# Attention, MLP and a Sinkhorn-gated MoE on one core: the right side of SBUF moved by 32 bytes, and TensorE's order in the MoE written out by hand

## The chip, the core and the metric

One core of a Trainium2 chip. Times are device microseconds of one execution of the whole program, and the lower the better. A profiled execution is recorded by the hardware profiler; its span is the stretch from the first to the last recorded instruction.

## The reference

Three layers, one after the other, in fp32:

```python
# attention: batch 4, 8 heads, 576 tokens, head width 64, mask by blocks of 64
scores = scale * np.matmul(q, k.transpose(0, 1, 3, 2))
scores = np.where(block_i >= block_j, scores, -1000000000.0)
attn = softmax(scores)
x = (attn @ v), heads side by side            # 2304 tokens x 512
# MLP: w_in 512 x 2048, w_out 2048 x 512
h = x @ w_in
x = np.maximum(0.01 * h, h) @ w_out
# MoE: 8 experts, w1 512 x 1024, w2 1024 x 512, every token in every expert
P = np.exp(x @ w_gate - max)                  # 2304 x 8
for _ in range(8):
    P /= P.sum(1, keepdims=True) + 1e-09
    P /= P.sum(0, keepdims=True) + 1e-09
    P *= N / E
for e in range(E):
    out += P[:, e:e + 1] * (np.maximum(x @ w1[e], 0.0) @ w2[e])
```

## The kernel before

Every fp32 matrix is split into a high and a low part (`...h`, `...l`), and one product is three matmuls: high by high, high by low, low by high. ScalarE (ACT) casts the high part, VectorE (DVE) subtracts to get the low one. The attention takes the first 250 us, the MLP the time up to about 676 us, and the MoE the rest.

**The MLP.** `hidden` (L492) multiplies a block of w_in with 512 or 384 tokens (five blocks of tokens: three of 512, two of 384), `second` (L514) adds the product with w_out into four PSUM banks.

**The MoE.** The tokens come in three passes p of 768, each in two halves of 384. A group (p, e, i) is a pass, an expert e of 8 and a quarter i of its hidden width: 96 groups. In a group the 2 x 2 block product x @ w1 is done with seven block products and sums instead of eight, named by the weight that they use: A11, S1, S2, S4, S3, A12, A22. Each is six matmuls (L672) of 128 x 384 into a PSUM bank. Bank X takes A11, S2, S3, A22 in turn, Y takes S1 and S4, Z takes A12. Between them ScalarE copies X (`s1`, `s2`) and Y (`s5`) out of PSUM, and VectorE adds such a copy to a later state of a bank: c12 = Y + s2, c11 = Z + s1, c22 = X + s5. From these ScalarE and VectorE make the high and low part of h11, h12, h22 (relu); h21 comes from X after A22. So A22 has to come after c22 has read X, S2 after s1, S3 after s2, S4 after s5.

Two groups share one `combine`, for each of six tiles of 128 tokens: twelve matmuls 128 x 512 (L708) that multiply h with w2, into one of the o banks; VectorE then adds the bank, weighted by the gate, to `xa` (L721).

Weights come by SP's queue into raw buffers (`wraw`, two of them for w1 and w2 together): `w1_load` and `w2_load` issue the DMA, which waits until the buffer's last reader is done. POOL makes the sums of w1's blocks (`one`, `two`), ScalarE casts w1h and w2h, VectorE subtracts w1l and w2l. `x_step` splits one of the seven x operands of a pass (`xhS..`, `xlS..`, ScalarE L659 and VectorE L660), five of them after a subtraction on POOL or from x itself; at the last group of a pass it makes those of the next pass. The eight rounds of the gate's normalisation (`rows`, `columns`) run in the first groups of the MoE; `columns` has a small matmul with `ones` that needs `cs` from VectorE, and its bank is read into `cr`.

The framework's scheduler sets the order of each engine's instructions, from the order in which the code emits them and its own estimates of their length. `alloc_tile_pool(..., side="right")` places a pool from the upper end of SBUF downward; other pools lie on the left side. On the right lie the split x of the attention and MLP (`xh`, `xl`), later the split x of the MoE (`xpart`) and h11, h12, h21 (`hpool1`).

Of the kernel before, what the change touches and what calls it, by code (L numbers as in the profile page):

```python
# [8 lines left out]
F32 = mybir.dt.float32  # L9
# [27 lines left out]
def block_attention_mlp_moe(  # L37
# [37 lines left out]
    const = ctx.enter_context(tc.tile_pool(name="const", bufs=1))  # L75
    xpool = tc.alloc_tile_pool(name="xpool", bufs=1, side="right")
# [452 lines left out]
    turn_o = [0]  # L529
# [6 lines left out]
    def gate_part(p, t0, n, ps):  # L536
        for t in range(t0, t0 + n):
            for c in range(KC):
                nc.tensor.matmul(  # L539
                    ps[:, t * E:(t + 1) * E], xv[p][:, c, t * P:(t + 1) * P], gate[:, c, :],  # L540
                    start=c == 0, stop=c == KC - 1,
                )

    def gate_take(p, ps):
# [4 lines left out]
    def gate_pass(p):  # L549
        ps = ps_h.tile([P, 512], F32, name="l_ps", tag="h")  # L550
        gate_part(p, 0, TC, ps)
        gate_take(p, ps)
# [51 lines left out]
    def w1_steps(n):  # L604
        if n >= NGR:
            return []
        _, e, i = groups[n]
        t = {}

        def sums():  # L610
            raw = w_raw.pop((1, NG + e, i)).rearrange("p (c f) -> p c f", c=KC)
            a11, a12, a21, a22 = (raw[:, c:c + 2, f:f + P] for f in (0, P) for c in (0, 2))
            one, two = (
                rawpool.tile([P, 512], F32, name="wa", tag="wa").rearrange("p (s c f) -> p s c f", s=2, c=2)
                for _ in range(2)
            )
            nc.gpsimd.tensor_tensor(out=one[:, 0], in0=a21, in1=a22, op=ALU.add)  # L617
            nc.gpsimd.tensor_tensor(out=one[:, 1], in0=one[:, 0], in1=a11, op=ALU.subtract)  # L618
            nc.gpsimd.tensor_tensor(out=two[:, 0], in0=a11, in1=a21, op=ALU.subtract)  # L619
            nc.gpsimd.tensor_tensor(out=two[:, 1], in0=a12, in1=one[:, 1], op=ALU.subtract)  # L620
            for k in "SA":
                for s in "hl":
                    t[k + s] = w1pool.tile([P, 1024], F32R, name=f"w1{s}", tag=f"w1{s}").rearrange(
                        "p (s c f) -> p s c f", s=4, c=2
                    )
            t["raw"], t["one"], t["two"] = raw, one, two
            for s, (k, j) in {"S1": "S0", "S2": "S1", "S3": "S2", "S4": "S3",
                              "A11": "A0", "A12": "A1", "A22": "A2"}.items():
                wq[n, s] = (t[k + "h"][:, int(j)], t[k + "l"][:, int(j)])

        def part(k, a, b, src):
            def run():
                x = src()
                hi, lo = t[k + "h"][:, a:b], t[k + "l"][:, a:b]
                if k == "A" and b - a == 2:
                    hi, lo = (y.rearrange("p s c f -> p (s c) f") for y in (hi, lo))
                elif k == "A":
                    hi, lo = hi[:, 0], lo[:, 0]
                nc.scalar.copy(out=hi, in_=x)  # L639
                nc.vector.tensor_tensor(out=lo, in0=x, in1=f32(hi), op=ALU.subtract)  # L640
            return run

        return [
            sums,
            part("A", 0, 2, lambda: t["raw"][:, :, 0:P]),
            part("A", 2, 3, lambda: t["raw"][:, 2:4, P:2 * P]),
            part("S", 0, 2, lambda: t["one"]),
            part("S", 2, 4, lambda: t["two"]),
        ]
# [14 lines left out]

    def product(n, k, name, first):
        if first:
            bank[n, name] = ps_h.tile([P, 512], F32, name="h_ps", tag="h")
        ps = bank[n, name][:, 0:HT]
        (wh, wl), (bh, bl) = wq.pop((n, k)), bq[groups[n][0], k]
        for c in range(2):  # L670
            for s, (w, x) in enumerate(((wh, bh), (wh, bl), (wl, bh))):
                nc.tensor.matmul(  # L672
                    ps, w[:, c], x[:, c], start=first and c == 0 and s == 0, stop=c == 1 and s == 2,
                    skip_group_check=True,
                )
# [19 lines left out]

    def combine(n, t):
# [50 lines left out]
    for m, (e, b, f) in enumerate(todo):  # L747
# [11 lines left out]
        if last and e + 1 == NG:  # L759
            if f == 1:  # L760
                w1_load(0)
                w2_load(0)
            if f == 3:
                for s in w1_steps(0):
                    s()
                w1_load(1)
        if e == 0 and b == 0:
            if f < len(late):
                bits_load(*late[f])
            if 0 < f <= len(late):  # L770
# [15 lines left out]
    hpool1 = tc.alloc_tile_pool(name="hpool1", bufs=3, side="right", reuse_waits="tile")  # L786
    mpool = tc.alloc_tile_pool(name="mpool", bufs=1, reuse_waits="tile")
# [5 lines left out]
    g_ps = {}  # L793

    def gate_last(t0):
        if t0 == 0:
            g_ps[0] = o_bank()
        gate_part(2, t0, 2, g_ps[0])
        if t0 + 2 == TC:
            gate_take(2, g_ps[0])  # L800

    for k in terms:
        x_step(0, k)

    def tail(n):
        product(n, "A22", "X", False)
        quarter(n, "21", "X", None)
        if groups[n][0] + 1 < NPASS and groups[n][1:] == (E - 1, NI - 1):
            x_step(groups[n][0] + 1, "A22")

    for n, (p, e, i) in enumerate(groups):
        turn = p + 1 < NPASS and (e, i) == (E - 1, NI - 1)
        if n >= 2:
            back = n - 2 - n % 2
            units = [lambda t=t: combine(back, t) for t in (range(TC // 2, TC) if n % 2 == 0 else range(TC // 2))]
        elif n == 0:
            units = [lambda t0=t0: gate_last(t0) for t0 in (0, 2, 4)]
        else:
            units = [lambda: None] * 3
        prep = w1_steps(n + 1)  # L820

        def prepare(m):
            for s in prep[:m]:
                s()
            del prep[:m]

        def normal():
            if n and norm:
                norm.pop(0)()

        def done(k):
            if turn:
                x_step(p + 1, k)
# [10 lines left out]
        prepare(1)  # L844
        normal()
        units[1]()
        prepare(1)
        product(n, "S1", "Y", True)
        keep(n, "Y", "s5")
        done("S1")  # L850
        product(n, "S2", "X", False)
        keep(n, "X", "s2")
        prepare(1)
        normal()
        units[2]()
        prepare(2)
        w1_load(n + 2)
        normal()
        product(n, "A12", "Z", True)
        quarter(n, "11", "Z", "s1")  # L860
        done("A12")
        done("S2")
        product(n, "S4", "Y", False)
        quarter(n, "12", "Y", "s2")
        done("S4")
        product(n, "S3", "X", False)
        quarter(n, "22", "X", "s5")
# [39 lines left out]
```

## Time and profile before

| | us |
|---|---|
| median of 3 runs | 2213.59 (2213.29 to 2216.33) |
| the profiled execution | 2214.53 |
| its span | 2212.7 |
| TensorE busy | 2185.7 (99%) |
| VectorE busy | 1320.0 (60%) |
| ScalarE busy | 899.5 (41%) |
| POOL busy | 471.9 (21%) |

A busy share says how long an engine had an instruction in it. Matmuls follow one another before the one ahead has left the array, so their recorded lengths overlap; what a matmul takes of the time is seen from one start to the next.

### The profile page before, as it was taken

To read this page: it belongs to the slowest core of one execution; us is meant where nothing else is said; L and a number is where in the kernel's file an instruction comes from. 1 tells how busy PE (TensorE), PEld (TensorE's weight loads), DVE (VectorE), ACT (ScalarE), POOL (GpSimd) and SP (SyncE) were. 2 spreads that over 40 slices of the span, in tenths; PEclk is the share of its full clock that TensorE was granted. 3 is DMA by queue.
4 is the path that set the end of the run, shared out by engine and by line. 5 is a ranking of instruction groups with operands and counts; after the bars stand their busy time and mean duration, and the time that the engine had idled before them with its cause. 6 is when DMAs were issued, how large, how long until landed. Compare 5 with 4: busy or idle time off the path is not lost.

```text
span 2212.7 us, 29298 instructions
## 1 busy us (share of the span) xinstructions
PE 2185.7 (99%) x10992; PEld 1932.6 (87%) x10992; DVE 1320.0 (60%) x2429; ACT 899.5 (41%) x1902; POOL 471.9 (21%) x547
## 2 busy tenths in 40 slices
PE   7999999999999999999999999999999999999999
PEld 6787777988899988898889888888898888888888
DVE  7999776333237856555557555555557555555554
ACT  6777422332124433443344334433444344334432
POOL 3433322000004121212123212121213121212120
PEclk9999999999999999999999999999999999999999
DMA  4333134010001212221222122212222222122211
GB/s 103 88 85 84 44 115 143 21 56 1 1 20 58 66 58 77 67 67 58 77 67 96 58 77 67 68 57 77 67 68 81 81 68 67 58 76 67 68 57 39
DMA packets 157246, 146.61 MB, mean 66 GB/s; under 512 B 62640, under 2 KB 126128, under 8 KB 157104
## 3 DMA queue, kind: packets, MB, share of 16 engines
q1 hardware_dynamic: 157104, 144.75, 22.2%
q8 instruction: 86, 1.41, 0.3%
q14 instruction: 56, 0.46, 0.1%
HBM read 135.81 MB, written 8.91 MB: 65 GB/s over the span
## 4 chain that ended last, share of the span: by engine, by line
PE 83%; POOL 0%; ACT 0%; DVE 0%; issue 0%; POOLq 0%; ACTq 0%
PE o L708 36%; PE h_ps L672 32%; PE h_ps L492 7%; PE o L514 7%; PE l_ps L539 1%; PE o L539 0%; POOL xa L657 0%; POOL wa L618 0%; POOL wa L617 0%; PE o L574 0%; POOL wa L619 0%; ACT xhS L659 0%; DVE xa L721 0%; DVE w1l L640 0%; ACT w1h L639 0%
## 5 line engine op out<-in xcount | busy, mean ns | idle before, releaser
L708 PE MATMUL o<-w2h,h 128*128 128x512 f32 x2304 | 767.6, 394 | 0.0
L708 PEld LDWEIGHTS o<-w2h,h 128*128 128x128 f32 x2304 | 431.6, 188 | 82.0
L708 PE MATMUL o<-w2l,h 128*128 128x512 f32 x1152 | 455.4, 396 | 0.0
L617 POOL TENSOR_TENSOR wa<-wraw 128x256 f32<-128x256 f32 x96 | 101.5, 1057 | 1394.6 <-DVE w1l L640 1305.6
L721 DVE SCALAR_TENSOR_TENSOR xa<-o,pr,xa 128x512 f32<-128x512 f32 x264 | 193.2, 746 | 172.1 <-PE o L708 172.0
L690 ACT ACTIVATE h<-c 128x384 fp32r<-128x384 f32 x288 | 151.2, 525 | 323.3 <-DVE c L685 318.1
L672 PE MATMUL h_ps<-xhS,w1h 128*128 128x384 f32 x768 | 261.4, 341 | 2.0 <-ACT xhS L659 2.0
L672 PE MATMUL h_ps<-xhS,w1l 128*128 128x384 f32 x768 | 261.4, 340 | 0.0
L672 PE MATMUL h_ps<-xlS,w1h 128*128 128x384 f32 x768 | 261.2, 340 | 0.0
L640 DVE TENSOR_TENSOR w1l<-wa,w1h 128x512 fp32r<-128x512 f32 x192 | 125.5, 695 | 213.1 <-ACT w1h L639 213.1
L708 PEld LDWEIGHTS o<-w2l,h 128*128 128x128 f32 x1152 | 216.2, 188 | 38.0
L639 ACT CAST w1h<-wa 128x512 fp32r<-128x512 f32 x192 | 109.6, 618 | 330.4 <-PE h_ps L672 326.2
L119 DVE TENSOR_TENSOR w2l<-wraw,w2h 128x1024 fp32r<-128x1024 f32 x100 | 127.6, 1276 | 176.0 <-ACT w2h L118 176.0
L679 ACT COPY s<-h_ps 128x384 f32<-128x384 f32 x288 | 136.9, 475 | 158.6 <-PE h_ps L672 158.6
L672 PE MATMUL h_ps<-xhA,w1h 128*128 128x384 f32 x576 | 195.5, 339 | 0.0
L672 PE MATMUL h_ps<-xlA,w1h 128*128 128x384 f32 x576 | 195.5, 339 | 0.0
L672 PE MATMUL h_ps<-xhA,w1l 128*128 128x384 f32 x576 | 195.5, 339 | 0.0
L685 DVE TENSOR_TENSOR c<-h_ps,s 128x384 f32<-128x384 f32 x288 | 160.0, 556 | 46.6 <-ACT h L690 25.7
L691 DVE SCALAR_TENSOR_TENSOR h<-c,h 128x384 fp32r<-128x384 f32 x288 | 158.7, 551 | 0.2
L672 PEld LDWEIGHTS h_ps<-xhS,w1h 128*128 128x128 f32 x768 | 144.9, 189 | 8.5 <-ACT xhS L659 2.3
L672 PEld LDWEIGHTS h_ps<-xlS,w1h 128*128 128x128 f32 x768 | 144.9, 189 | 7.9
L672 PEld LDWEIGHTS h_ps<-xhS,w1l 128*128 128x128 f32 x768 | 145.0, 189 | 1.9
(131 smaller groups left out, 3666.4 us busy)
## 6 DMA issues: line engine op xcount, KB each, us to landing
wraw<-in_moe_w_dram SPq DMA_DIRECT2D x192, 512.0 KB, 3.7
wraw<-in_moe_w_in_dram SPq DMA_DIRECT2D x16, 512.0 KB, 3.9
wraw<-in_moe_w_out_dram SPq DMA_DIRECT2D x16, 512.0 KB, 3.6
out_dram<-xa SPq DMA_DIRECT2D x18, 256.0 KB, 2.0
qraw<-in_q_dram SPq DMA_DIRECT2D x32, 128.0 KB, 2.5
kraw<-in_k_dram SPq DMA_DIRECT2D x32, 128.0 KB, 2.7
vz<-in_v_dram SPq DMA_DIRECT2D x32, 128.0 KB, 2.4
s_in<-wa SPq DMA_DIRECT2D x8, 256.0 KB, 3.1
```

The source lines that it names most:

```text
L119: nc.vector.tensor_tensor(out=lo, in0=raw, in1=f32(hi), op=ALU.subtract)
L492: nc.tensor.matmul(ps[:, 0:n], w[:, c, cols], x, start=c == 0 and s == 0, stop=c == KC - 1 and s == 2,)
L514: nc.tensor.matmul(o_ps[s][:, 0:n], w[:, cut], h[:, 0:n], start=f == 0 and m == 0, stop=f == FC - 1 and m == 2)
L639: nc.scalar.copy(out=hi, in_=x)
L640: nc.vector.tensor_tensor(out=lo, in0=x, in1=f32(hi), op=ALU.subtract)
L672: nc.tensor.matmul(ps, w[:, c], x[:, c], start=first and c == 0 and s == 0, stop=c == 1 and s == 2, skip_group_check=True,)
L679: nc.scalar.copy(out=t, in_=bank[n, name][:, 0:HT])
L685: nc.vector.tensor_tensor(out=c, in0=x, in1=part[n, add], op=ALU.add)
L690: nc.scalar.activation(out=hi, in_=x, func=AF.Relu)
L691: nc.vector.scalar_tensor_tensor(out=lo, in0=x, scalar=0.0, in1=f32(hi), op0=ALU.max, op1=ALU.subtract)
L708: nc.tensor.matmul(o, h, w, start=m == 0, stop=m == 11)
L721: nc.vector.scalar_tensor_tensor(out=a, in0=o, scalar=pr[:, tt, e:e + 1], in1=a, op0=ALU.mult, op1=ALU.add)
```

## The change

- A tile of 8 floats (32 bytes) is placed first on the right side, so that all that follows on that side lies 32 bytes lower.
- In the MoE TensorE's instructions follow the order of the code: `in_order` puts each `product`, `combine` and the gate's last pass behind the last matmul of the one before (`issue_after`). The other engines' order stays with the scheduler.
- The order in a group: A11, S1, A22 of the group before, S2, S4, S3, A12. After an even group (i even, not the first of a pass) come the six combines of the two groups before it. In the last group of a pass A22 of the same group follows A12, and the combines of the group before and this one follow that, with the next pass's x_steps between them. Before, combines stood three to a group between the products, and the scheduler could move them.
- PSUM: the banks of the products go round over five (`h_bank`), those of the combines over three (`o_bank`); before it was four and four.
- `s1` has a pool of its own with two buffers. The two parts of w1 (`w1_a`, `w1_s`) have tiles made separately, at other places in the group; w2's split and the next w2's load stand at the group's end instead of behind A11. The gate of pass 3 is one piece in front of the first group instead of three pieces inside it.

```diff
+    edge = tc.alloc_tile_pool(name="edge", bufs=1, side="right")
+    edge.tile([P, 8], F32, name="edge")
...
     def o_bank():
-        s = turn_o[0] % 4
+        s = turn_o[0] % 3
...
+    def h_bank():
+        turn_h[0] += 1
+        if turn_h[0] % 5 == 0:
+            return ps_o.tile([P, 512], F32, name="o3", tag="o3")
+        return ps_h.tile([P, 512], F32, name="h_ps", tag="h")
...
+    last_mm = [None]
+
+    def in_order(f):
+        def run(*a):
+            with ExitStack() as order:
+                if last_mm[0] is not None:
+                    order.enter_context(tc.issue_after(last_mm[0]))
+                ins = f(*a)
+            last_mm[0] = ins.ins if hasattr(ins, "ins") else ins
+        return run
...
+    order = [*range(TC // 2, TC), *range(TC // 2)]
     for n, (p, e, i) in enumerate(groups):
...
         product(n, "A11", "X", True)
         keep(n, "X", "s1")
-        done("A11")
-        w2_split(n)
-        w2_load(n + 1)
-        normal()
-        units[0]()
-        if n:
-            tail(n - 1)
...
+        product(n, "S1", "Y", True)
+        keep(n, "Y", "s5")
+        if (e, i) != (0, 0):
+            tail(n - 1)
+        w1_a(n + 1)
+        w1_load(n + 2)
+        if 0 < n < 6:
+            normal()
+            normal()
+        product(n, "S2", "X", False)
+        keep(n, "X", "s2")
+        product(n, "S4", "Y", False)
+        quarter(n, "12", "Y", "s2")
+        product(n, "S3", "X", False)
+        quarter(n, "22", "X", "s5")
+        if 0 < n < 6:
+            normal()
+            normal()
+        product(n, "A12", "Z", True)
+        quarter(n, "11", "Z", "s1")
         w2_split(n)
         w2_load(n + 1)
-        normal()
-        units[0]()
...
+        w1_sums(n + 2)
+        if turn:
+            tail(n)
+            back = n - 1
+        elif i % 2 == 0 and (e, i) != (0, 0):
+            back = n - 2
+        else:
+            back = None
+        if back is not None:
+            for m, t in enumerate(order):
+                combine(back, t)
+                if turn and p + 1 < NPASS:
+                    for k in terms[2 * m:2 * m + 2]:
+                        x_step(p + 1, k)
+                if m == 1:
+                    w1_s(n + 2)
+        else:
+            w1_s(n + 2)
...
```

What the scheduler makes of it, at three places. First ScalarE in the middle of a pass, from the cast of a group's w2 (`w2h`) to the copy `s2` of the next, even group; now:

```order
L121 CAST w2h_11168<-wraw_11077 128x1024
L693 COPY s1_11098<-h_ps_11091 128x384
L704 ACTIVATE h11_11070<-c11_11068 128x384
L693 COPY s5_11107<-o3_11100 128x384
L646 CAST w1h_11118<-wraw_11029 128x512
L646 CAST w1h_11118<-wraw_11029 128x256
L704 ACTIVATE h21_11115<-h_ps_10996 128x384
L693 COPY s2_11132<-h_ps_11091 128x384
```

and before:

```order
L118 CAST w2h_10362<-wraw_10225 128x1024
L679 COPY s1_10219<-h_ps_10212 128x384
L690 ACTIVATE h22_10209<-c22_10207 128x384
L639 CAST w1h_10256<-wa_10250 128x512
L639 CAST w1h_10256<-wa_10251 128x512
L690 ACTIVATE h21_10247<-h_ps_10075 128x384
L679 COPY s5_10283<-h_ps_10276 128x384
L679 COPY s2_10291<-h_ps_10212 128x384
```

Between the cast of w2 and `s2` stand the same kinds of operation; the cast of w1's A part (from `wraw`) has come in for that of its S part (from `wa`), and h11 for h22.

Second VectorE at the first turn, from c12 of the last group of pass 1 to the low part of its h22; now:

```order
L699 TENSOR_TENSOR c12_10459<-o3_10419,s2_10451 128x384
L671 TENSOR_TENSOR xlS4_10578<-xa1_2967,xhS4_10577 128x768
L699 TENSOR_TENSOR c22_10470<-h_ps_10410,s5_10426 128x384
L671 TENSOR_TENSOR xlS1_10529<-xa1_2967,xhS1_10528 128x768
L699 TENSOR_TENSOR c11_10482<-h_ps_10475,s1_10417 128x384
L705 SCALAR_TENSOR_TENSOR h12_10461<-c12_10459,h12_10461 128x384
L647 TENSOR_TENSOR w1l_10557<-wa_10493,w1h_10556 128x512
L647 TENSOR_TENSOR w1l_10557<-wa_10494,w1h_10556 128x512
L671 TENSOR_TENSOR xlA12_10548<-xa1_2967,xhA12_10547 128x768
L671 TENSOR_TENSOR xlS3_10583<-xa1_2967,xhS3_10582 128x768
L122 TENSOR_TENSOR w2l_10705<-wraw_10491,w2h_10704 128x1024
L705 SCALAR_TENSOR_TENSOR h22_10472<-c22_10470,h22_10472 128x384
```

and before:

```order
L685 TENSOR_TENSOR c12_10488<-h_ps_10417,s2_10437 128x384
L660 TENSOR_TENSOR xlA12_10474<-xa1_2963,xhA12_10473 128x768
L685 TENSOR_TENSOR c22_10503<-h_ps_10349,s5_10424 128x384
L660 TENSOR_TENSOR xlS4_10494<-xa1_2963,xhS4_10493 128x768
L691 SCALAR_TENSOR_TENSOR h11_10470<-c11_10468,h11_10470 128x384
L640 TENSOR_TENSOR w1l_10566<-wraw_10459,w1h_10565 128x512
L640 TENSOR_TENSOR w1l_10566<-wraw_10459,w1h_10565 128x256
L660 TENSOR_TENSOR xlS3_10510<-xa1_2963,xhS3_10509 128x768
L691 SCALAR_TENSOR_TENSOR h12_10490<-c12_10488,h12_10490 128x384
L119 TENSOR_TENSOR w2l_10668<-wraw_10526,w2h_10667 128x1024
L691 SCALAR_TENSOR_TENSOR h22_10505<-c22_10503,h22_10505 128x384
```

c22 stands behind one `xl` in both; behind it and ahead of h22 there are now the low part of w1's S part, three `xl`, c11, h12 and w2l, where before there were h11, the A part, one `xl`, h12 and w2l.

Third VectorE in the normalisation, from a round's first sums over rows to `cs`; now, in group 4:

```order
L579 TENSOR_REDUCE rs_2975<-pr_2970 128x18
L122 TENSOR_TENSOR w2l_6920<-wraw_6733,w2h_6919 128x1024
L580 TENSOR_SCALAR rs_2975<-rs_2975 128x18
L705 SCALAR_TENSOR_TENSOR h11_6726<-c11_6724,h11_6726 128x384
L731 TENSOR_TENSOR xa0_2966<-o2_6741,xa0_2966 128x512
L647 TENSOR_TENSOR w1l_6770<-wa_6735,w1h_6769 128x512
L581 RECIPROCAL rs_2975<-rs_2975 128x18
L647 TENSOR_TENSOR w1l_6770<-wa_6736,w1h_6769 128x512
L582 TENSOR_TENSOR pr_2970<-pr_2970,rs_2975 128x144
L585 TENSOR_REDUCE cs_2976<-pr_2970 128x8
```

and such a round of before:

```order
L564 TENSOR_REDUCE rs_2971<-pr_2966 128x18
L565 TENSOR_SCALAR rs_2971<-rs_2971 128x18
L640 TENSOR_TENSOR w1l_6216<-wa_6209,w1h_6215 128x512
L566 RECIPROCAL rs_2971<-rs_2971 128x18
L685 TENSOR_TENSOR c22_6288<-h_ps_6183,s5_6230 128x384
L640 TENSOR_TENSOR w1l_6216<-wa_6210,w1h_6215 128x512
L691 SCALAR_TENSOR_TENSOR h21_6206<-h_ps_6071,h21_6206 128x384
L567 TENSOR_TENSOR pr_2966<-pr_2966,rs_2971 128x144
L119 TENSOR_TENSOR w2l_6462<-wraw_6306,w2h_6461 128x1024
L685 TENSOR_TENSOR c12_6277<-h_ps_6223,s2_6238 128x384
L691 SCALAR_TENSOR_TENSOR h22_6290<-c22_6288,h22_6290 128x384
L570 TENSOR_REDUCE cs_2972<-pr_2966 128x8
```

In both a w2l stands inside the round; now it is behind the row sums and ahead of all the rest of it.

## Rows read from the trace of the kernel before

**Rows 1.** The page's head: span, and busy time, share and instructions by engine.

```profile
span 2212.7 us, 29298 instructions
...
PE 2185.7 (99%) x10992; PEld 1932.6 (87%) x10992; DVE 1320.0 (60%) x2429; ACT 899.5 (41%) x1902; POOL 471.9 (21%) x547
```

**Rows 2.** Windows: stretch, its length, busy by engine, granted clock, DMA share, GB/s.

```profile
681.03:684.61 3.58, 3.58 (x11) 3.58 (x12) 3.58 (x3) 0.69 (x1) 2.86 (x2) 0.52 0.43 146
720.00:2208.00 1488.00, 1488.00 (x7348) 1334.40 (x7347) 874.42 (x1467) 587.00 (x1131) 307.57 (x372) 1.00 0.22 68
```

**Rows 3.** TensorE's timeline in the MoE: start, length, engine, line, operation.

```profile
1399.06 0.34 PE L672 MATMUL h_ps<-xhS,w1h 128*128 128x384 f32 x1
...
1402.23 0.40 PE L708 MATMUL o<-w2h,h 128*128 128x512 f32 x1
...
1410.97 0.40 PE L708 MATMUL o<-w2h,h 128*128 128x512 f32 x1
...
1413.77 0.34 PE L672 MATMUL h_ps<-xhA,w1h 128*128 128x384 f32 x1
```

**Rows 4.** TensorE's timeline in the MLP, 462 to 470 us.

```profile
462.72 0.34 PE L514 MATMUL o<-hh,w2h 128*128 128x384 f32 x1
...
464.80 0.40 PE L492 MATMUL h_ps<-xh,w1h 128*128 128x512 f32 x1
...
468.08 0.39 PE L514 MATMUL o<-hh,w2h 128*128 128x512 f32 x1
...
469.48 0.39 PE L492 MATMUL h_ps<-xh,w1l 128*128 128x512 f32 x1
```

**Rows 5.** TensorE's timeline earlier in the MLP, 342 to 345 us.

```profile
342.54 0.39 PE L514 MATMUL o<-hh,w2h 128*128 128x512 f32 x1
...
344.57 0.39 PE L492 MATMUL h_ps<-xh,w1h 128*128 128x512 f32 x1
```

**Rows 6.** ScalarE's timeline in the MoE; in brackets idle time before and its releaser.

```profile
1417.16 0.91 ACT L639 CAST w1h<-wraw 128x512 fp32r<-128x512 f32 x2
1417.98 0.52 ACT L690 ACTIVATE h<-c 128x384 fp32r<-128x384 f32 x1
...
1434.51 1.05 ACT L118 CAST w2h<-wraw 128x1024 fp32r<-128x1024 f32 x1 [0.70 <-DMA wraw<-in_moe_w_dram]
1435.47 0.47 ACT L679 COPY s<-h_ps 128x384 f32<-128x384 f32 x1
```

**Rows 7.** VectorE's timeline in the same stretch: the low part of w1's A part.

```profile
1418.09 1.02 DVE L640 TENSOR_TENSOR w1l<-wraw,w1h 128x512 fp32r<-128x512 f32 x2
```

**Rows 8.** SP's queue in the same stretch: the load of w2.

```profile
1430.71 0.37 SPq L103 DMA_DIRECT2D wraw<-in_moe_w_dram  x1
```

**Rows 9.** VectorE's timeline at the first turn of a pass.

```profile
1182.94 2.42 DVE L660 TENSOR_TENSOR xlS<-xa,xhS 128x768 fp32r<-128x768 f32 x1
...
1186.68 0.95 DVE L660 TENSOR_TENSOR xlS<-xa,xhS 128x768 fp32r<-128x768 f32 x1
1187.55 0.55 DVE L691 SCALAR_TENSOR_TENSOR h<-c,h 128x384 fp32r<-128x384 f32 x1
1188.02 1.22 DVE L119 TENSOR_TENSOR w2l<-wraw,w2h 128x1024 fp32r<-128x1024 f32 x1
...
1189.62 1.29 DVE L640 TENSOR_TENSOR w1l<-wa,w1h 128x512 fp32r<-128x512 f32 x2
```

**Rows 10.** ScalarE's and TensorE's timeline at the start of the MoE.

```profile
680.15 0.83 ACT L659 CAST xhS<-xa 128x768 fp32r<-128x768 f32 x1 [2.82 <-POOL xa L657]
...
681.03 0.61 PE L672 MATMUL h_ps<-xhS,w1h 128*128 128x384 f32 x1 [1.99 <-ACT xhS L659]
...
681.44 0.52 PE L672 MATMUL h_ps<-xhA,w1h 128*128 128x384 f32 x1
```

**Rows 11.** VectorE's timeline in the normalisation.

```profile
697.15 0.27 DVE L566 RECIPROCAL rs<-rs 128x18 f32<-128x18 f32 x1
...
698.15 0.43 DVE L570 TENSOR_REDUCE cs<-pr 128x8 f32<-128x144 f32 x1
```

More of the change, by code (lines that the diff above doesn't have):

```diff
@@ L547, in gate_take @@
         )
[L549 to L552, printed above, removed]
+        return mm
     def gate_max():
@@ L602, in w2_split, with w1_sums @@
             w_split(2, NG + groups[n][1], groups[n][2])
-    def w1_steps(n):
+    wt = {}
+    def w1_sums(n):
         if n >= NGR:
[L606 to L648, printed above, removed]
-        ]
@@ new lines, in w1_sums @@
+            return
+        raw = w_raw.pop((1, NG + groups[n][1], groups[n][2])).rearrange("p (c f) -> p c f", c=KC)
+        a11, a12, a21, a22 = (raw[:, c:c + 2, f:f + P] for f in (0, P) for c in (0, 2))
+        one, two = (
+            rawpool.tile([P, 512], F32, name="wa", tag="wa").rearrange("p (s c f) -> p s c f", s=2, c=2)
+            for _ in range(2)
+        )
+        nc.gpsimd.tensor_tensor(out=one[:, 0], in0=a21, in1=a22, op=ALU.add)
+        nc.gpsimd.tensor_tensor(out=one[:, 1], in0=one[:, 0], in1=a11, op=ALU.subtract)
@@ new lines, in w1_sums, with w1_tiles @@
+        nc.gpsimd.tensor_tensor(out=two[:, 0], in0=a11, in1=a21, op=ALU.subtract)
+        nc.gpsimd.tensor_tensor(out=two[:, 1], in0=a12, in1=one[:, 1], op=ALU.subtract)
+        wt[n] = (raw, one, two)
+    def w1_tiles(n, names):
+        t = [
+            w1pool.tile([P, 1024], F32R, name=f"w1{s}", tag=f"w1{s}").rearrange("p (s c f) -> p s c f", s=4, c=2)
+            for s in "hl"
+        ]
+        for j, k in enumerate(names):
+            wq[n, k] = tuple(x[:, j] for x in t)
+        return t
@@ new lines, in halves, with w1_s, w1_a @@
+    def halves(hi, lo, x):
+        nc.scalar.copy(out=hi, in_=x)
+        nc.vector.tensor_tensor(out=lo, in0=x, in1=f32(hi), op=ALU.subtract)
+    def w1_s(n):
+        if n < NGR:
+            t = w1_tiles(n, ("S1", "S2", "S3", "S4"))
+            for j, x in ((0, wt[n][1]), (2, wt[n][2])):
+                halves(*(y[:, j:j + 2] for y in t), x)
+    def w1_a(n):
+        if n < NGR:
+            t = w1_tiles(n, ("A11", "A12", "A22"))
+            raw = wt.pop(n)[0]
+            halves(*(y[:, 0:2].rearrange("p s c f -> p (s c) f") for y in t), raw[:, :, 0:P])
+            halves(*(y[:, 2] for y in t), raw[:, 2:4, P:2 * P])
@@ L786, in block_attention_mlp_moe @@
     hpool1 = tc.alloc_tile_pool(name="hpool1", bufs=3, side="right", reuse_waits="tile")
+    spool = tc.alloc_tile_pool(name="spool", bufs=2, side="right", reuse_waits="tile")
     mpool = tc.alloc_tile_pool(name="mpool", bufs=1, reuse_waits="tile")
@@ L807, in tail, with normal @@
         quarter(n, "21", "X", None)
-        if groups[n][0] + 1 < NPASS and groups[n][1:] == (E - 1, NI - 1):
-            x_step(groups[n][0] + 1, "A22")
+    def normal():
+        if norm:
+            norm.pop(0)()
+    order = [*range(TC // 2, TC), *range(TC // 2)]
     for n, (p, e, i) in enumerate(groups):
[L812 to L833, printed above, removed]
+        turn = (e, i) == (E - 1, NI - 1)
         product(n, "A11", "X", True)
         keep(n, "X", "s1")
-        done("A11")
+        product(n, "S1", "Y", True)
+        keep(n, "Y", "s5")
+        if (e, i) != (0, 0):
+            tail(n - 1)
```

69 lines of the change are left out of this document (22 added, 47 removed).

## Prediction

> **What bounds the kernel now.** I read the page first. The span is 2212.7 us and TensorE is busy for 2185.7 us of it [rows 1]. The profiled execution took 2214.53 us, 1.83 more than its span and 0.94 above the median of 2213.59. The windows by stage come next. From 720 to 2208 us, nearly all of the MoE, PE is busy in all of 1488.00 us at a granted clock of 1.00 [rows 2]. So in the MoE only two things count: how far apart TensorE starts its matmuls, and whether an edit makes it wait, since no wait is left there to be won back.
>
> For the spacing I took starts from TensorE's timeline, not the busy means, which overlap. Three products of 18 matmuls on 384 columns go from 1399.06 to 1402.23: 176.1 ns each. A combine of 12 on 512 columns takes 1410.97 to 1413.77: 233.3 ns [rows 3]. In the first MLP the 12 matmuls of L514 on 384 columns, 462.72 to 464.80, are 173.3 ns apart. L492's 14 on 512 columns, up to 468.08, are 234.3 apart, and L514's 6 on 512, up to 469.48, 233.3 [rows 4]. Other L514 matmuls on 512 columns, 9 from 342.54 to 344.57, are 225.6 apart [rows 5].
>
> **What the addresses say.** In the built program every right-side tile starts 32 bytes past a multiple of 64 (the split x of L492 and of the products; part of the h of a combine); L514 reads only multiples of 64. That goes with 173.3 against 176.1 on 384 columns. On 512 columns aligned reads have both spacings. The 225.6 of rows 5 belongs to stationary and moving tiles that lie an odd or twice odd multiple of 512 bytes apart; the 233.3 of rows 4 is aligned too, but not a multiple of 512 apart. The 8-float tile of the diff moves the right side to multiples of 64.
>
> **The gains.** Products: 4032 x 2.8 ns = **-11.3 us** (0 if address has nothing to do with it; -13 if the other matmuls of the class gain a little more). Combines: 480 of 3456 come to lie at the distances of rows 5, so 480 x 7.7 ns = **-3.7** (0 to 3456 x 7.7 = -26.6; I take the small value because aligned matmuls in rows 4 still need 233.3). Hidden layer L492: 576 on 512 columns x 1.0 ns and 384 on 384 columns x 2.8 = **-1.6** (0 to -6). With 2.8 ns off, a product takes 6 x 173.5 = 1.041 us.
>
> The Trainium skill (SBUF — State Buffer, Operand start alignment) asks only that an operand starts at a multiple of its element size, and calls that a rule of legality, not speed. The same page's specifications give SBUF lines of 16 bytes, of which 32 bytes are two whole ones. By that page an offset of 32 bytes would cost nothing and these three terms would be 0; the 176.1 against 173.3 speaks against it.
>
> **Costs: the even groups.** TensorE no longer goes by what is ready. In each group it issues A11, S1, A22 of the group before, S2, S4, S3, A12. Between S2 and S3, which share a bank, stood two products; now only S4 stands there. S3 waits until ScalarE has copied s2. Let T be the start of A11 in an odd group; the even group's S3 is 12 products later, at T + 12.49. The chain against it: ScalarE casts the A part of the next w1 when three products are done, T + 3.20 with a hop of 0.08. VectorE's low part follows 0.65 later (the first of the two casts, two thirds of 0.91 [rows 6], and a hop) and takes 1.02 [rows 7], T + 4.87. It frees the raw buffer for SP's load of w2 (0.05). From SP's issue at 1430.71 to the cast of w2 at 1434.51 is 3.80 us [rows 6, 8], so that cast starts at T + 8.72. Behind it on ScalarE, in order (excerpt of the change), stand s1, h11, s5, the w1 pair, h21 and s2. From start to start [rows 6] the cast of w2 holds ScalarE 0.96, a copy 0.37 (0.47 less 0.1 of overlap), h11 0.43, the pair 0.82; h21, also out of a bank, like a copy with 0.39, and s2 with its full 0.48. At 681.03 TensorE started 0.05 after the operation it waited for had ended (680.15 + 0.83), and its next matmul came about 0.1 late, 0.41 after it against 0.32 [rows 10]: with 0.16 for going on, that is 3.98: T + 12.70, 0.21 late. 45 pairs have it: **+9.5** (0 if the load lands 0.2 sooner; 18 if 0.4 late). Odd groups have six combines (16.8 us) as cover, and nothing is late there.
>
> **Costs: the two turns of a pass.** At (e 7, i 3) A22 of the same group stands one product after S3, on the bank that c22 reads; before, the next group's A11 and a combine lay between. On VectorE c22 is behind xlS4, which took 2.42 us where another xl took 0.95 [rows 9]. The wait is 2.42 + 0.55 for c22 (like h) + 0.16 + 0.05 for a hop - 1.05 for A12 = 2.1. Then the last matmul of the first combine needs the low half of h22 of this same group. VectorE's line up to it: xlS1 0.87, c11 0.47, h12 0.47, w1 pair 1.20, xlA12 0.87, xlS3 0.87, w2l 1.13, h22 0.55 = 6.43 (each as in [rows 9], less 0.08 for overlap). TensorE is there after A22 and eleven matmuls, 1.05 + 11 x 0.233 = 3.61: with 0.16 a wait of 3.0. Two turns: 2 x 5.1 = **+10.2** (3.4 if xlS4 runs alone in 0.95 and the rest half as long, to 13.6).
>
> **Costs: the normalisation.** Its eight matmuls with `ones` were put anywhere; now the scheduler sets them between combines. One stands right behind the first combine of group 4, at T + 10.08 (T is A11 of group 4; seven products and a combine of 2.79). It needs `cs`. VectorE has w2l ahead of that chain, which waits for the same load: T + 8.72 + 1.08 = 9.80. Then w2l 1.13, h11 0.47, w1l 1.20, the eviction some 0.68 (h's 0.55 by 512 columns, less overlap), rs, reciprocal and pr 0.25 each from the reciprocal's 0.27, and cs 0.43 [rows 9, 11]: 4.66. TensorE goes on at T + 14.6, 4.5 late. The next round through nine such short operations (9 x 0.27 = 2.4) and its hops (0.5) has no more cover: **+7.4** (2 to 9).
>
> **Costs: the start of the MoE.** The gate of pass 3 comes in one piece, and TensorE may not go past it. By the order of VectorE and ScalarE there, TensorE waits some 1.4 (the MLP's last low half behind an xl of the x-steps, 2.42 as in rows 9 less a product), 0.9 (gate behind the last addition to x, an eviction and a hop), 2.3 (s1 on ScalarE behind exp, which waits for POOL's maximum: eight short operations) and 0.3 more. These are estimates; of their 4.9, 1.99 was there before [rows 10]: **+2.9** (0 to 5). **The clock.** After the wait of 1.99 at 681.03 [rows 10] TensorE took 3.58 us for 11 matmuls worth 1.94 at the spacing of rows 3, at a granted clock of 0.52 [rows 2], the lower of its two levels (1.2 for 2.4 GHz): it lost 1.6. Three more waits of 2 us or longer lose some 1.5 each: **+4.6** (0, to 7.5 if five do).
>
> **At nothing:** h banks over five and o banks over three (a bank of o comes round after 8.4 us, and VectorE's longest operation in rows 9 is 2.42); s1 twice; w1's tiles made apart; SP's order, which waits for VectorE's release of a raw buffer either way. Were that cover gone, the cost would be the turn's own (2.1 each).
>
> **Sum:** 2214.5 - 16.6 + 9.5 + 10.2 + 7.4 + 2.9 + 4.6 = 2232.5 for a profiled execution, 2231.6 for the median.
>
> **Rivals.** *Combines gain too (the other side):* all 3456 come down to 225.6 as in rows 5, because the 233.3 of rows 4 has another cause than the distance. 22.9 us more off: 2208.7. It decides below a mean of some 226.5 ns. Chance 0.15. *The waits do not show:* the load lands 0.2 us sooner, so S3 and the `ones` matmul find their data, and xlS4 takes 0.95. Then some 5 of 34.6 us are left: 2202, and with half the turns left 2207. For it: 0.21 us is small against 12.49. Against it: the lines at the turns are lines of whole operations in a fixed order. Chance 0.13. *Alignment does nothing:* the 2.8 ns belong to L514's other tiles. The waits stay: 2231.6 + 16.6 = 2248. For it: aligned matmuls with 512 columns show 233.3 as well. Chance 0.11. My forecast has 0.61; its own range is 2217 to 2241.
>
> **The numbers.** A change under 0.2% (4.4 us) can hardly be told from none. Faster, below 2209.2: most of the first two rivals, 0.22. Within, 2209.2 to 2218.0: their rest and the forecast's low end, 0.14. Slower: 0.64. The range, 2204 to 2246, takes in the waits not showing and nearly the case without gain from alignment.
>
> **What would show it.** Products 173 to 174 ns apart and combines 231 to 232. Waits of TensorE in 720 to 2208: 45 at an even group's S3 ended by ScalarE's s2, a pair at each of the two turns ended by VectorE's c22 and h22, some in the first five groups ended by cs. A clock below 1.00 after them. I am wrong if that window again has no waits, or if a combine takes 2.71 us.

## The result and the profile after

The changed kernel takes 2245.4 us (median of 4 runs, 2240.4 to 2246.7) where the kernel before took 2213.4 beside it (4 runs, 2212.6 to 2216.3): 1.0138 times as long, 95% interval 1.0119 to 1.0156. It is slower by 32 us; the forecast had 2231.6. The profiled execution took 2246.74 us, 1.7 more than its span.

The head of the page of after, which answers to [rows 1]:

```profile
span 2245.0 us, 29156 instructions
...
PE 2190.0 (98%) x10992; PEld 1926.5 (86%) x10992; DVE 1340.7 (60%) x2429; ACT 884.7 (39%) x1902; POOL 467.4 (21%) x547
```

TensorE has as many matmuls as before and hardly more busy time; the loss doesn't show in its share. It shows in the windows of after, with the columns of [rows 2]:

```profile
681.00:698.00 17.00, 16.93 (x78) 16.93 (x79) 11.21 (x21) 3.40 (x6) 4.58 (x3) 0.60 0.09 32
698.00:790.00 92.00, 84.85 (x426) 76.06 (x425) 65.49 (x150) 39.67 (x80) 16.27 (x21) 0.96 0.20 59
720.00:2240.00 1520.00, 1493.79 (x7357) 1328.49 (x7356) 892.88 (x1463) 571.49 (x1130) 306.67 (x372) 0.99 0.21 67
1180.00:1210.00 30.00, 22.99 (x99) 19.69 (x98) 22.72 (x26) 13.52 (x23) 11.63 (x8) 0.89 0.18 62
1194.32:1196.41 2.09, 2.09 (x7) 2.09 (x7) 2.09 (x3) 2.09 (x4) 1.20 (x1) 0.50 0.37 141
1210.00:1700.00 490.00, 488.32 (x2424) 435.60 (x2423) 286.21 (x464) 184.77 (x368) 99.00 (x125) 1.00 0.22 69
1700.00:1740.00 40.00, 33.18 (x148) 28.77 (x148) 26.71 (x32) 15.38 (x27) 11.54 (x8) 0.91 0.26 92
```

Where [rows 2] had no idle time at all, 720 to 2240 has 26 us of it. The first groups (698 to 790, with the normalisation) and the two turns (1180 to 1210, 1700 to 1740) each have some 7 us of idle time and a clock below 1.00. Between the turns 490 us hold only 1.7 us idle. The table of TensorE's waits says what ended them (line waited for: us in all, times, longest):

```profile
PE o L723 <- DVE h L705: 8.3, 2, 4.2
...
PE o L589 <- DVE cs L585: 4.9, 1, 4.9
PE h_ps L684 <- ACT s L693: 3.8, 8, 1.0
...
PE h_ps L684 <- DVE c L699: 2.8, 1, 2.8
PE o L684 <- DVE c L699: 2.8, 1, 2.8
PE o L684 <- ACT s L693: 2.2, 2, 1.2
```

The turns are h (h22's low half) and c (c22), once each per turn; cs is the normalisation; s the even groups' copies, of which only ten waits are long enough to be listed. TensorE's timeline of after gives the spacing, as [rows 3] did:

```profile
1383.67 0.34 PE L684 MATMUL o<-xhA,w1h 128*128 128x384 f32 x1
...
1386.79 0.34 PE L684 MATMUL o<-xhS,w1h 128*128 128x384 f32 x1
...
1398.30 0.40 PE L723 MATMUL o<-w2h,h 128*128 128x512 f32 x1
...
1415.03 0.33 PE L684 MATMUL h_ps<-xhA,w1h 128*128 128x384 f32 x1
```

Eighteen matmuls of products in 3.12 us are 173.3 ns each (176.1 before). Seventy-two of the combines in 16.73 us are 232.4 (233.3 before).

I then took all 10992 starts of TensorE in both profiled executions. From each interval between two starts I took the class's usual spacing; what is left over in a stretch is called its excess below. It holds waits, late starts and half clock together. Times in us:

| term | forecast | measured |
|---|---|---|
| products, 4032 | -11.3 | 4032 x (173.48 - 176.56 ns) = -12.4 |
| combines, 3456 | -3.7 | 3456 x (232.15 - 232.70 ns) = -1.9 |
| MLP up to its last L492 matmul | -1.6 (spacing) | -1.3 (by the spacing alone -3.3) |
| even groups (pairs) | +9.5 | +13.0 |
| two turns | +10.2 | +20.8 |
| normalisation | +7.4 | +10.6 |
| start of the MoE | +2.9 | +3.7 |
| lower clock | +4.6 | in the four above |
| sum | +18.0 | +32.5; the spans differ by 32.3 |

### The profile page after: what moved, and what is told of

Read it like the earlier page. It is cut to its first block, busy times and chain, and to the rows that moved or that the text cites. A ratio compares the mean times of both kernels' runs of the same rounds, so it can differ in the third digit from the quotient of the medians.

```text
span 2245.0 us, 29156 instructions
## 1 busy us (share of the span) xinstructions
PE 2190.0 (98%) x10992; PEld 1926.5 (86%) x10992; DVE 1340.7 (60%) x2429; ACT 884.7 (39%) x1902; POOL 467.4 (21%) x547
## 4 chain that ended last, share of the span: by engine, by line
PE 79%; DVE 2%; DMA 2%; ACT 1%; issue 1%; SPq 0%; ACTq 0%; DVEq 0%
PE o L723 35%; PE h_ps L684 23%; PE h_ps L495 7%; PE o L517 7%; PE o L684 6%; DMA wraw<-in_moe_w_dram 2%; DVE w1l L647 1%; PE l_ps L560 1%; PE o L560 0%; DVE w2l L122 0%; ACT w1h L646 0%; DVE h L705 0%; ACT s L693 0%; ACT w2h L121 0%; DVE xlA L671 0%
## 5 line engine op out<-in xcount | busy, mean ns | idle before, releaser
L723 PE MATMUL o<-w2h,h 128*128 128x512 f32 x2304 | 734.4, 396 | 9.8 <-DVE h L705 8.3
L684 PE MATMUL h_ps<-xhS,w1h 128*128 128x384 f32 x616 | 211.4, 343 | 4.0 <-ACT s L693 3.8
L684 PE MATMUL h_ps<-xlS,w1h 128*128 128x384 f32 x616 | 207.5, 337 | 0.0
L684 PE MATMUL h_ps<-xhS,w1l 128*128 128x384 f32 x616 | 207.4, 337 | 0.0
L647 DVE TENSOR_TENSOR w1l<-wraw,w1h 128x512 fp32r<-128x512 f32 x192 | 106.5, 595 | 120.4 <-ACT w1h L646 120.4
L684 PE MATMUL h_ps<-xhA,w1h 128*128 128x384 f32 x462 | 156.2, 338 | 2.8 <-DVE c L699 2.8
L121 ACT CAST w2h<-wraw 128x1024 fp32r<-128x1024 f32 x100 | 105.0, 1050 | 133.2 <-DMA wraw<-in_moe_w_dram 131.3
L684 PE MATMUL h_ps<-xhA,w1l 128*128 128x384 f32 x462 | 156.1, 338 | 0.0
L684 PE MATMUL h_ps<-xlA,w1h 128*128 128x384 f32 x462 | 156.1, 338 | 0.0
L503 DVE TENSOR_TENSOR g<-h_ps,g 128x512 f32<-128x512 f32 (+1 forms) x80 | 50.7, 634 | 126.9 <-ACT g L502 126.7
```

Source lines behind the costliest of these rows:

```text
L121: nc.scalar.copy(out=hi, in_=raw)
L684: mm = nc.tensor.matmul(ps, w[:, c], x[:, c], start=first and c == 0 and s == 0, stop=c == 1 and s == 2, skip_group_check=True,)
L723: mm = nc.tensor.matmul(o, h, w, start=m == 0, stop=m == 11)
```

## The experiments

The ratio of each is to the kernel before, run beside it on the same chip (medians 2214.6 for the first four, 2214.3 for the next four, 2216.8 for the last three).

**The address alone, and the rest of the change alone.** The first is the kernel before with the 32-byte tile and nothing else, the second the changed kernel without it, that is the order together with its banks, pools and the gate in one piece.

```diff
+    edge = tc.alloc_tile_pool(name="edge", bufs=1, side="right")
+    edge.tile([P, 8], F32, name="edge")
```

> The kernel before with the 32-byte tile alone; no engine's order changes. Theory (the address of the moving operand sets the spacing): products 173.5 instead of 176.6 ns, combines 232.2 instead of 232.7, the hidden layer 1.3 us shorter in sum: 15.6 us less than before, 2198 (2194 to 2202). Rival (the closer spacing came with the new order of TensorE or the other banks): no change, 2213. A half-way result, some 2206, would say that only the products gain.

> The changed kernel without the 32-byte tile: the new order alone. Theory (order and address add up): 15.6 us more than the changed kernel, less what the slower products hide of the waits (up to 5 us): 2256 to 2261. Rival (the address does nothing): 2245.

Measured: address alone 2196.4, ratio 0.9917 (0.9902 to 0.9933); the rest alone 2257.9, 1.0193 (1.0174 to 1.0212), both within what was expected. So the address wins 18 us and the rest loses 43 (what of these 43 is the order and what its banks and pools wasn't run apart); with the new order the address is worth 2257.9 - 2245.4 = 12.5. TensorE's timeline with the address alone, in the MoE and in the MLP, and its window:

```profile
463.34 0.40 PE L494 MATMUL h_ps<-xh,w1h 128*128 128x512 f32 x1
...
466.56 0.40 PE L516 MATMUL o<-hh,w2h 128*128 128x512 f32 x1
...
1389.96 0.33 PE L674 MATMUL h_ps<-xhA,w1h 128*128 128x384 f32 x1
...
1394.12 0.39 PE L710 MATMUL o<-w2h,h 128*128 128x512 f32 x1
```

```profile
720.00:2190.00 1470.00, 1470.00 (x7324) 1320.22 (x7324) 870.39 (x1461) 585.44 (x1129) 308.05 (x372) 1.00 0.22 69
```

Twenty-four matmuls of products in 4.16 us are 173.3 ns each, and the hidden layer's fourteen in 3.22 are 230.0, with no idle time in 1470 us. Over the whole execution the products' mean is 173.6 and the combines' 232.1, as in after. That is 11.9 + 2.1 us, and the hidden layer's usual spacing gives 384 x 3.2 + 576 x 3.6 ns = 3.3 more: 17.3 us. The two profiled executions lie only 15.4 apart, since waits and slow stretches elsewhere, most of them in the MLP, are some 2 us longer in sum. This kernel and the one with 96 bytes below are the shortest of all kernels here.

**The turn.** The changed kernel, with the x_steps at a turn emitted behind h22's two halves on ScalarE and VectorE.

```diff
-                    for k in terms[2 * m:2 * m + 2]:
-                        x_step(p + 1, k)
+                    with ExitStack() as behind:
+                        for ins in made["22"]:
+                            behind.enter_context(tc.issue_after(ins.ins if hasattr(ins, "ins") else ins))
+                        for k in terms[2 * m:2 * m + 2]:
+                            x_step(p + 1, k)
```

> The changed kernel, but at the two turns of a pass VectorE and ScalarE make the next pass's x operands only behind h22 (c22 and h22 no longer stand behind the xl). Theory (the turn's waits are VectorE's line): 2 x 7.3 us of waits and some 2.5 us of lower clock behind each go: 20 us less, 2225 (2222 to 2230). Rival (the x operands are then late for the next pass's first products, or TensorE waits for w1 instead): half or more comes back, 2235 to 2245.

Measured: 2228.1, ratio 1.0055 (1.0039 to 1.0072), 17.3 us below after. The excess at the two turns went from 20.8 to 0.3 us: what stood ahead of c22 and h22 at the turns were these steps and what they slow down. In the table of this kernel's waits neither h nor c stands any more. But some 3.9 us came back at each of the two places behind, the first group of passes 2 and 3, 7.8 in all. S2 waits there for ScalarE's s1, which stands behind the cast of an x operand of the new pass (xhA), one of the steps that were moved, and that cast waits for POOL's subtraction. So the rival of this experiment holds in part. ScalarE and TensorE of this kernel at the start of pass 2:

```profile
1210.05 0.83 ACT L670 CAST xhA<-xa 128x768 fp32r<-128x768 f32 x1 [2.63 <-POOL xa L668]
1210.79 0.85 ACT L693 COPY s<-h_ps 128x384 f32<-128x384 f32 x2
...
1211.32 0.44 PE L684 MATMUL h_ps<-xhS,w1h 128*128 128x384 f32 x1 [2.06 <-ACT s L693]
```

Of the 17.3 us, 2.5 lie ahead of the MoE, whose first product starts at 688.23 instead of 690.74 us; the edit changes nothing there, and why isn't shown.

**The even groups' copy.** ScalarE's cast of w2 in an odd group is put behind the next group's s2, so that a late load can no longer hold up s1 and s2.

```diff
-        keep(n, "X", "s2")
+        s2 = keep(n, "X", "s2")
+        if late_w2:
+            with tc.issue_after(s2):
+                w2_split(n - 1)
+            w2_load(n)
...
-        w2_split(n)
-        w2_load(n + 1)
+        late_w2 = i % 2 == 1 and not turn
+        if not late_w2:
+            w2_split(n)
+            w2_load(n + 1)
```

> The changed kernel, but ScalarE casts an odd group's w2 only behind the copy s2 of the next group, so that s1, s5 and s2 no longer stand behind the load of w2; the load after it is issued later too. Theory (S2 and S3 of even groups wait for copies queued behind a load of varying length): some 11 of 13.4 us of these waits go, 2234 (2231 to 2238). Rival (the late w2 or the raw buffers make something else late, as w1's sums or the combine): 2242 to 2250.

Measured: 2301.4, ratio 1.0387 (1.0372 to 1.0403). My forecast for it fell. The rival there (the raw buffers) holds in kind, but cost far more than its 2250 at most: the pairs' excess is 67 us, not near 0. The timelines of this kernel, from SP's queue to TensorE:

```profile
1410.70 8.88 SPq L101 DMA_DIRECT2D wraw<-in_moe_w_dram  x2
...
1416.87 0.62 ACT L646 CAST w1h<-wa 128x512 fp32r<-128x512 f32 x1 [0.96 <-POOL wa L631]
...
1419.64 0.44 PE L684 MATMUL h_ps<-xhS,w1h 128*128 128x384 f32 x1 [1.18 <-ACT s L693]
```

A w2 that is cast later keeps its raw buffer. The load of the next w1 then waits on SP for the other one until VectorE's w1l has read it, POOL's sums and ScalarE's w1h come late, and s2 stands behind w1h. S3 waits 1.1 to 1.5 us in most pairs, and up to 2.8 in a few, instead of now and then.

**A third raw buffer.** w2 gets a raw buffer of its own (s1 gives up one of its two to make room), and its cast is put behind the same group's h11.

```diff
+        pool, tag = (rawpool, "wraw") if which == 1 or not third else (third[0], "wraw3")
...
-        w2_split(n)
+        h11 = made["11"][0]
+        with tc.issue_after(h11.ins if hasattr(h11, "ins") else h11):
+            w2_split(n)
```

> The changed kernel with a third raw buffer, for w2 alone (s1 goes back to one buffer to make room), and the cast of w2 on ScalarE behind its own group's h11. Loads of w1 and w2 no longer wait for each other's buffers, so the load of w2 is done before ScalarE comes to its cast. Theory (S2 and S3 wait for copies behind a late load): the 13 us of short waits in the pairs go, 2233 (2230 to 2237). Rival (ScalarE's line is too long by itself, load or not; or one s1 buffer makes new waits): 2243 or more.

Measured: 2267.1, ratio 1.0246 (1.0227 to 1.0264): 22 us slower than after, a miss of 34. The waits of 0.4 to 1.4 us behind a late load no longer come up through the passes; early in each pass one pair still waits for s1, 1.2 to 3.0 us. But the turns now cost 15.3 to 15.9 us each: a combine waits for w2l, at the end of VectorE's line. And in about each fifth pair A12 waits 1.0 us until VectorE has read its bank for the low half of an h. The pairs' excess is 23 us, more than the 13 of after. The waits and one such pair in the timelines:

```profile
PE o L726 <- DVE w2l L123: 17.0, 3, 8.1
```

```profile
1409.76 0.55 DVE L707 SCALAR_TENSOR_TENSOR h<-o,h 128x384 fp32r<-128x384 f32 x1
...
1410.36 0.44 PE L685 MATMUL o<-xhA,w1h 128*128 128x384 f32 x1 [0.99 <-DVE h L707]
```

**Without the normalisation.** The changed kernel with `SINKHORN = 0`: it leaves out the eight rounds of the normalisation, so its time is that of a smaller computation.

> The changed kernel without the eight rounds of the normalisation (gate values are only exponentials; the output is not the reference's). Theory (the matmuls with ones wait for cs and cr, with lower clock behind it): the waits of the first five groups go, 10 us less, 2235 (2233 to 2238). Rival (these groups wait for w2, h and the loads, and the small operations only stood in their line): 2242 to 2245.

Measured: 2231.4, ratio 1.0079 (1.0057 to 1.0102). The excess of the first six groups, 13.97 in after, fell to 3.86: 10.1 us are the normalisation's. The other 4 of the 14.0 us below after lie elsewhere: the MoE's first product starts 2.5 us earlier, the pairs have some 3 us less excess and the turns some 2 more.

**Three repairs at once.** The third raw buffer as above, the turn's repair, and the normalisation's matmuls with `ones` placed between chosen products and combines by hand (excerpt).

```diff
-        norm += [rows, columns]
+        norm += [rows, in_order(columns)]
```

> The changed kernel with the turn as in the experiment on it, the third raw buffer, and the ones matmuls placed by hand (one at the end of a group of products, two among the combines of groups 2 and 4, their sums started some 5 us ahead). Theory (the waits are separate and add up): 17 + 12 + 8 us less than the changed kernel, 2208 (2203 to 2213), which leaves the MoE's start as the main loss against the kernel before with the tile alone. Rival (a fixed order makes TensorE wait somewhere in any case, waits move): 2220 or more.

Measured: 2253.7, ratio 1.0182 (1.0162 to 1.0201): a miss of 46; the waits moved, as the rival had it. The third buffer again had combines at the turns wait for w2l (15.2 us in 3 waits), and the first groups, with the normalisation, had some 4 us more excess than in after.

**What of the address counts.** The kernel before with the tile widened to 64, 96 and 128 bytes (16, 24, 32 floats). With 64 and 128 the right side lies 32 bytes past a multiple of 64 as before; with 96 on a multiple.

> The kernel before with a tile of 64 bytes in place of 32: the right side moves but lies again 32 bytes past a multiple of 64. Theory (the address modulo 64 of the moving operand sets the spacing): products 176.5 ns, 2213 as before. Rival (any move helps, since it is the distance to the weights on the left that counts): 2196 to 2205.

> The kernel before with a tile of 96 bytes: the right side lies again at multiples of 64, but 64 bytes lower than with 32. Theory (multiples of 64 give the close spacing): products 173.5 ns, 2196 to 2199. Rival (what counts is how far x lies from the weights on the left, modulo 512: 96, 64, 32 and now 0 bytes): products at 175 or more, 2203 or more, as the 64-byte tile gave 2203.9.

> The kernel before with a tile of 128 bytes: the right side 32 bytes past a multiple of 64, as before and as with 64 bytes. Theory (modulo 64 alone): products 176.5 ns, 2213. The 64-byte tile gave 2203.9 with hidden-layer matmuls at 176.2 and 232.7 ns as before, but products at 174.4. Rival (a second effect of the place, on products alone): 2200 to 2208 again.

Measured: 64 bytes 2203.9, ratio 0.9959 (0.9946 to 0.9973); 96 bytes 2197.6, 0.9916 (0.9899 to 0.9932); 128 bytes 2203.5, 0.9937 (0.9917 to 0.9957). Both multiples of 64 agree within 1.2 us. But 64 and 128 bytes don't give the time of before back: that it is the remainder by 64 alone fell. TensorE's timeline with 64 bytes, in the MLP and at two places 16 us apart:

```profile
463.57 0.40 PE L494 MATMUL h_ps<-xh,w1h 128*128 128x512 f32 x1
...
466.84 0.39 PE L516 MATMUL o<-hh,w2h 128*128 128x512 f32 x1
...
1389.53 0.34 PE L674 MATMUL h_ps<-xhA,w1h 128*128 128x384 f32 x1
...
1393.77 0.39 PE L710 MATMUL o<-w2h,h 128*128 128x512 f32 x1
...
1405.26 0.34 PE L674 MATMUL h_ps<-xhA,w1h 128*128 128x384 f32 x1
...
1409.42 0.39 PE L710 MATMUL o<-w2h,h 128*128 128x512 f32 x1
```

The hidden layer's fourteen are 233.6 apart, slow as before; the first 24 products 4.24/24 = 176.7 ns, and 24 others of the same kernel 4.16/24 = 173.3. So off a multiple of 64 the products run in stretches at either spacing; what picks the stretch stays open. The hidden layer's 512 columns do follow the remainder: their mean is 229.5 to 229.6 ns on a multiple of 64 (32 and 96 bytes, and after) and 232.5 to 233.3 off it (no tile, 64 and 128 bytes).

**Turn and pairs together.** The turn's repair, a third raw buffer for w2, and w2's cast behind the next group's s2 as in the fourth experiment.

```diff
+        pool, tag = (rawpool, "wraw") if which == 1 or not third else (third[0], "wraw3")
...
+        if late_w2:
+            with tc.issue_after(s2):
+                w2_split(n - 1)
+            w2_load(n)
```

> The changed kernel with the turn of e3, a third raw buffer for w2, and an odd group's w2 cast behind s2 of the next group as in e4: now neither the load nor the cast of w2 stands ahead of s1, s5 and s2, and w1 has both old buffers. Theory (waits at S2 and S3 are this line on ScalarE): 17 us less from the turns and some 10 from the pairs, 2218 (2214 to 2224). Rival (SP's queue issues w1 behind w2's loads, so that w1's sums come late and S3 waits some 1.2 us a pair as in e4): 2240 or more.

Measured: 2216.3 (10 runs), ratio 1.0000 (0.9991 to 1.0010). The pairs' excess fell from 13.0 to 3.8 and the turns' from 20.8 to 1.7. What stays is the normalisation's `cs` (the line below) and the start of the MoE:

```profile
PE o L590 <- DVE cs L586: 6.5, 2, 5.3
```

That supports the load and the buffer as the pairs' cause: with a buffer to spare, the same late cast that cost 54 us more in the pairs now wins 9. With two of the four costs nearly gone the written order is no better than the scheduler's at the old address; at the new address the scheduler's is some 18 us ahead (ratio 0.9917).

## Why the prediction came out as it did

**The sign and the sum's build were right.** The address gains and the written order costs more. The time lies inside the range, 0.6 below its upper end, and 4 us beyond the forecast's own range. The room that it fell into had been left for alignment doing nothing, not for dearer waits, so that it lies inside is in part luck. The gains were -16.6 forecast and -15.6 measured, the costs +34.6 and +48.1. The miss is in the costs.

**Products** held: -12.4 for -11.3, shown by the address alone. The Trainium skill (SBUF — State Buffer, Operand start alignment) speaks of legality and not of speed, and so gives an offset of 32 bytes no price. Here it has one: 2214.6 against 2196.4.

**Combines** were half of the term: -1.9 for -3.7, and its reason was wrong. 480 of them were to come to the distances of [rows 5]. In the built program of before, 480 lay at them already (all with h22) and took 232.6 ns; the 480 of after take 231.3, not 225.6, and the other 2976 gained 0.4 ns each. In the MLP's L514 the distance does go with the spacing: before, the 324 matmuls on 512 columns at those distances took 226.7, the 252 others 232.6. The rival that all combines come down (2208.7) is out, as is the one that alignment does nothing.

**The hidden layer** gained twice its term in spacing: 384 x 3.1 and 576 x 3.6 ns, 3.3 us, where I had 2.8 and 1.0 ns. Some 2 us of it went into longer waits and slow stretches of the MLP, whose last L492 matmul starts at 670.70 instead of 671.99 us.

**Even groups** were mis-sized by 3.5 us, and their form was wrong. I had 45 times 0.21 from one load's 3.80 us. In fact the usual pair costs 0 to 0.3, and eight pairs cost 0.7 to 1.8. SP, ScalarE and TensorE in a usual even group and in one of the eight, in after:

```profile
1388.56 0.37 SPq L106 DMA_DIRECT2D wraw<-in_moe_w_dram  x1
...
1392.25 1.05 ACT L121 CAST w2h<-wraw 128x1024 fp32r<-128x1024 f32 x1 [0.54 <-DMA wraw<-in_moe_w_dram]
...
1608.12 0.37 SPq L106 DMA_DIRECT2D wraw<-in_moe_w_dram  x1
...
1613.54 1.04 ACT L121 CAST w2h<-wraw 128x1024 fp32r<-128x1024 f32 x1 [2.27 <-DMA wraw<-in_moe_w_dram]
...
1615.02 0.44 PE L684 MATMUL o<-xhS,w1h 128*128 128x384 f32 x1 [1.23 <-ACT s L693]
```

From issue to cast the same transfer takes 3.69 us in the one and 5.42 in the other; the 93 of the execution go from 3.6 to 5.8. When it is late S2 waits for s1 already, not only S3 for s2. One row was the price of a transfer whose tail sets the cost.

**The turns are the step that failed in size**: 5.1 us of waits a turn forecast, 7.0 measured, and 10.4 with the late starts and the clock behind them. The mechanism and the place were right, shown by the repair that took 20.5 of 20.8 us away there (7.8 came back one group later). Wrong was VectorE's line, costed operation by operation from [rows 9]. POOL, VectorE and TensorE at the first turn of after:

```profile
1187.61 4.11 POOL L668 TENSOR_TENSOR xa<-xa 128x768 f32<-128x768 f32 x2 [9.36 <-DVE xlA L671]
1195.21 1.83 POOL L668 TENSOR_TENSOR xa<-xa 128x768 f32<-128x768 f32 x1 [3.49 <-DVE xlS L671]
1199.67 2.39 POOL L668 TENSOR_TENSOR xa<-xa 128x768 f32<-128x768 f32 x1 [2.64 <-DVE xlA L671]
```

```profile
1187.89 4.11 DVE L647 TENSOR_TENSOR w1l<-wraw,w1h 128x512 fp32r<-128x512 f32 x2 [0.36 <-ACT w1h L646]
...
1193.72 0.54 DVE L699 TENSOR_TENSOR c<-h_ps,s 128x384 f32<-128x384 f32 x1
...
1195.05 0.54 DVE L699 TENSOR_TENSOR c<-h_ps,s 128x384 f32<-128x384 f32 x1
1195.52 1.94 DVE L705 SCALAR_TENSOR_TENSOR h<-c,h 128x384 fp32r<-128x384 f32 x1
...
1200.32 2.82 DVE L122 TENSOR_TENSOR w2l<-wraw,w2h 128x1024 fp32r<-128x1024 f32 x1
```

```profile
1194.32 0.69 PE L684 MATMUL h_ps<-xhA,w1h 128*128 128x384 f32 x1 [2.79 <-DVE c L699]
...
1203.67 0.98 PE L723 MATMUL o<-w2h,h 128*128 128x512 f32 x2 [4.22 <-DVE h L705]
```

The low half at 1195.52 ends 0.42 after POOL's operation beside it, w2l 1.08 after its own: a VectorE operation with two inputs in SBUF does its work once POOL's is over. The pair w1l takes the 4.11 of POOL's pair, where it took 1.02 in [rows 7]. Over 1.02, 0.55 and 1.22 these three lost 3.1 + 1.4 + 1.6 = 6.1 us of VectorE's time at one turn. The c at 1195.05, with one input in PSUM, isn't stretched. This also explains the xlS4 of [rows 9], which I carried over as a length of its own; POOL's timeline of before has, at the same place:

```profile
1182.69 1.85 POOL L657 TENSOR_TENSOR xa<-xa 128x768 f32<-128x768 f32 x1 [4.55 <-DVE xlA L660]
```

Its 2.42 us began 0.25 into that operation and ended 0.82 after it. In after both xlS take 0.94, since POOL is idle beside them, and other operations pay. The Trainium skill (SBUF — State Buffer, Who interferes with whom) says just this: a VectorE instruction with two SBUF inputs contends with a GpSimd instruction that reads SBUF, one with at most one SBUF input, outside the two-port modes, doesn't, and the lock is exclusive. These rows agree.

**The normalisation** cost 10.6 us with its clock, 10.1 by the run without it, for 7.4 and a share of the 4.6. The wait itself was near the forecast: 4.87 us for `cs`, where I had 4.5.

```profile
756.32 0.60 PE L589 MATMUL o<-cs,ones 128*128 128x8 f32 x2 [4.87 <-DVE cs L585]
```

**The start of the MoE** was 3.7 for 2.9 and part of the clock, too near for a run of its own. The waits of 2.86 and 0.64 us ahead of 681 stand in the timeline, and the gate's 48 matmuls then took 9.8 us at a mean clock of 0.53 (681.07 to 690.74 us; the first window above, which holds them, has 0.60). The wait of some 2.3 at s1 that I had put there isn't seen: the first product follows the gate at once.

```profile
679.46 0.97 PE L517 MATMUL o<-hl,w2h 128*128 128x384 f32 x4 [2.86 <-DVE hl L505]
...
681.07 9.82 PE L560 MATMUL o<-gate,xa 128*128 128x8 f32 x48 [0.64 <-DVE xa L528]
690.74 0.67 PE L684 MATMUL h_ps<-xhA,w1h 128*128 128x384 f32 x1
```

**The clock** was right in kind: the seven matmuls from 1194.32 on, behind a wait of 2.79 us, ran at 0.50, the lower of the two levels. How the excess at a turn divides between clock and late starts wasn't measured apart.

**The rival that the waits do not show** is out for the sum. **At nothing** held for the banks of products, and nearly for those of o: combines waited 3 times, 1.5 us in all, for `cr` to read the bank of a `ones` matmul, within the normalisation's stretch.

## What to carry to other kernels

A bound engine's order written by hand makes each of its waits the price of the slowest load and the longest line ahead of it, so cost such waits by the spread of the transfers and not by one row. An operation's length read in one place holds at another only with the same neighbours: before carrying it over, look at what the engine that shares its port did at that time. Split a change that does two things at the first chance: here one half was worth 18 us and the other cost 43. And work that is moved away from one wait can make the next: of 20.5 us won at the turns 7.8 came back a group later.

## What the runs showed of the hardware

- The spacing of matmuls comes in levels 3.4 to 3.6 ns apart in these rows: 173.3 and 176.7 on 384 columns; 226.4, 230.0 and 233.6 on 512. The 226.4 is the hidden layer's fourteen with the 96-byte tile (463.06 to 466.23 us).
- A right side at multiples of 64 bytes kept the products' mean at 173.5 to 174.2 ns in three kernels. At 32 past, the means were 176.6 and 176.7 with no tile (before, and the rest of the change alone) and 174.6 and 174.7 with the 64- and the 128-byte one. What else decides is open. The hidden layer's 512 columns took 229.5 to 229.6 and 232.5 to 233.3.
- Loads of the same 512 KB took 3.6 to 5.8 us from issue to cast in one execution.
- VectorE's operations with two inputs in SBUF ended after the POOL operation beside them; one with an input in PSUM did not wait.
